# Own PSUM banks for y of the first four blocks, one product pair for the factors of all blocks, and a new order

## The chip, the cores and the metric

The kernel runs on one core of a Trainium2 chip. The metric is the device time in microseconds of one execution. A core has a matrix engine (PE), a vector engine (DVE), a scalar engine (ACT), a general engine (POOL), and a queue engine (SP) that here issues every transfer (DMA). Each engine works through its own list of instructions in order and waits on semaphores that the others raise.

## What is computed

Three steps follow one another: a chunked state-space scan over 32 sequences (batch 4, heads 8) of 768 tokens, and two gated feed-forward layers over the 3072 tokens.

```python
for c in range(nc):                                    # the scan, chunk by chunk
    L = np.exp(cum[:, :, :, None] - cum[:, :, None, :]) * causal
    M = np.einsum('bhin,bhjn->bhij', Cc, Bc) * L
    y_intra = np.einsum('bhij,bhjd->bhid', M, xc)
    y_inter = np.einsum('bhin,bhnd->bhid', Cc, state) * np.exp(cum)[:, :, :, None]
    y[:, :, sl] = y_intra + y_inter
    Bx = np.einsum('bhjn,bhjd->bhjnd', Bc, xc) * np.exp(cum[:, :, -1:] - cum)[:, :, :, None, None]
    state = np.exp(np.sum(la, axis=-1))[:, :, None, None] * state + np.sum(Bx, axis=2)

h = x @ w_in                                           # layer 1: 256 -> 2048 -> 256
x = (h * (1.0 / (1.0 + np.exp(-h)))) @ w_out
h = x @ w_in                                           # layer 2, other weights
g = (a[0] + a[1]*h + a[2]*h**2 + a[3]*h**3) / (1.0 + abs(b[0])*abs(h) + abs(b[1])*h**2 + 1e-06)
out = g @ w_out
```

The weights of both layers come as 64-bit floats. Operands of the layers are split into a high and a low part, and each product is taken as three (high by high, high by low, low by high).

## The kernel before, in words

The 3072 tokens are 24 blocks of 128. The scan runs block by block; layers 1 and 2 run over six groups of four blocks (512 tokens), and for each group over 16 slices f of 128 hidden units. Each slice is six products of 128x512 for h (`in_proj`) and six for the sum acc (`out_proj`). All products go through one helper, so every PE row of the profile has line 402.

The start of the program: la, cum and con (constants) are loaded; la is clipped (DVE, L478) and its logarithm taken (ACT, L479). `decays` makes eG and eL, per-token factors for each block, from products of la with cum (L496, L499, L513); it is called for blocks 0 to 3 and, later, for 4 to 23. `factors` makes Ea, factors along the chunk: for blocks 0 to 2 directly (lab, L565 or L567; product; exponential L552), for the others in two products for all blocks whose exponentials T (L552) are written to dre in DRAM (L576) and come back, repeated over partitions, as Ea (L688). Ea of block 3 comes alone, the others in groups of two to four.

One block of the scan: its data is loaded into tok (L675, six buffers); POOL multiplies B by eL (L713); DVE or POOL multiply C by Ea (L720, then L724); Gm is eG times a triangle (L699). PE makes CB (eight records of 64x128 from tok) and the chunk sums U (eight of 32x64), both in att, a PSUM tile of four banks. DVE makes M from CB and Gm (L768) and the states S (L787, L789). PE then makes y from M and x (x16) and from C and S (one or two times x8); ACT rounds it to y1h (L893) and DVE keeps the rest as y1l (L896). From block 5 on (`ALONE`), one "visit" of PE makes CB and U of the next block and y of this one. In att, each of CB, U and y has two places, by the block's parity, in the same four banks.

One weight slice of layer 1: the raw 64-bit words are loaded into wraw (L590, three buffers); ACT makes a scaled copy wv (L603), DVE shifts and joins the bits (L609, L611), ACT takes the high part w (L627) and POOL or DVE the low part (L631). Layer 2's weights take the same path into wraw, are written to DRAM (w2s) and reloaded later.

In a layer, ACT applies the gate (T, L976), ACT or POOL take gh (L935, L937) and DVE or POOL take gl (L941). PSUM has eight banks: four for att, two for acc, two for h (a ring that decays, factors and the layers share). Warm-up products of zeros (23 of 128x512, bf16) go into a bank of acc.

The order on every engine is set by a list scheduler in the kernel (`Plan.run`): each operation has a key, an estimated length and dependencies; at each step it takes, among those that could start first, the one with the lowest key. The keys come from a table, `first`, of one line per operation: its number, its key, and the time before which it isn't placed. `wr` and `rd` name the PSUM banks that an operation writes or reads, for the planner's estimate of when it can start. Names such as tok_101 carry a running number that differs between two versions: in the kernel before, tok_101, 106, 112 and 124 are blocks 0 to 3; in the changed one tok_113, 130, 133 and 143.

## Time and profile before

| what | us |
|---|---|
| median of 3 runs | 592.51 (591.71 to 593.67) |
| the profiled execution, its own time | 591.67 |
| its span, first to last instruction | 589.8 |
| PE busy | 577.5 |
| DVE busy | 434.7 |
| ACT busy | 405.7 |
| POOL busy | 301.5 |

The page gives busy time by engine over the whole span, then the chain of work that ended last, and the groups of instructions. PE is at 98% of the span, so what matters is where it waits and what it does before layer 1 begins. The views by stretch and in order of time show that.

### The profile page before, as it was taken

What the parts mean: (1) busy time and instruction counts of PE and PEld (TensorE: products, weight loads), DVE (VectorE), ACT (ScalarE), POOL (GpSimd) and SP (SyncE); (2) the same over time, 40 slices, a digit from 0 to 9 for tenths busy, and PEclk for the clock granted to TensorE, in tenths of its full rate; (3) what the DMA queues carried; (4) which work ended last, traced back from release to release, by engine and by line L of the source; (5) the groups of instructions that cost most, each with busy time, mean ns of one, the idle gap of its engine ahead of it and who ended that gap; (6) DMA issues with size and microseconds to landing.
All of it is one profiled execution on the core that took longest, in us unless ns stands there. A gap on an engine that the chain in (4) does not pass through costs nothing.

```text
span 589.8 us, 11914 instructions
## 1 busy us (share of the span) xinstructions
PE 577.5 (98%) x4589; PEld 463.8 (79%) x4589; DVE 434.7 (74%) x722; ACT 405.7 (69%) x728; POOL 301.5 (51%) x328
## 2 busy tenths in 40 slices
PE   7799999999999999999999999999999999999997
PEld 4477777777888888888888888888888888888885
DVE  4899999888522222222124999999999999999995
ACT  4466666456433544444446899989999999999994
POOL 4354416541112100100102788888888888888883
PEclk9799999999999999999999999999999999999999
DMA  7876566876300000000047500000000000000000
GB/s 249 260 238 229 199 198 241 293 234 221 144 1 0 1 0 1 1 1 0 1 138 230 203 1 1 37 1 1 36 1 2 37 1 0 36 2 2 36 2 36
DMA packets 16200, 48.84 MB, mean 83 GB/s; under 512 B 1872, under 2 KB 2960, under 8 KB 16144
## 3 DMA queue, kind: packets, MB, share of 16 engines
q1 hardware_dynamic: 16144, 48.09, 24.0%
q8 instruction: 36, 0.59, 0.4%
q14 instruction: 20, 0.16, 0.1%
HBM read 36.44 MB, written 11.64 MB: 82 GB/s over the span
## 4 chain that ended last, share of the span: by engine, by line
PE 87%; DVE 6%; DMA 3%; ACT 2%; SPq 1%; issue 1%; DVEq 0%; ACTq 0%
PE acc L402 42%; PE h L402 34%; PE b L402 8%; PE att L402 3%; DMA wraw<-in_w_dram 2%; DVE wv L611 1%; DVE w L631 1%; DVE wv L609 1%; DMA Ea<-dre 1%; DVE M L768 1%; ACT wv L603 1%; SPq L675 0%; DVE y1l L896 0%; ACT T L976 0%; DVE S L789 0%
## 5 line engine op out<-in xcount | busy, mean ns | idle before, releaser
L402 PE MATMUL h<-y1h,w 128*128 128x512 f32 x636 | 216.9, 391 | 0.4 <-ACT y1h L893 0.3
L402 PE MATMUL acc<-gh,w 128*128 128x512 f32 x768 | 207.1, 391 | 0.0
L402 PEld LDWEIGHTS acc<-gh,w 128*128 128x128 f32 x768 | 143.1, 188 | 30.6 <-ACT wraw L1100 0.3
L941 DVE TENSOR_TENSOR gl<-T,gh 128x512 fp32r<-128x512 f32 x85 | 59.7, 705 | 115.6 <-ACT gh L935 90.4
L402 PEld LDWEIGHTS h<-y1h,w 128*128 128x128 f32 x636 | 119.3, 188 | 26.9 <-ACT y1h L893 0.8
L941 POOL TENSOR_TENSOR gl<-g,gh 128x512 fp32r<-128x512 f32 x95 | 122.8, 1295 | 19.4 <-ACT gh L935 16.5
L402 PE MATMUL h<-y1l,w 128*128 128x512 f32 x318 | 123.9, 390 | 0.3 <-DVE y1l L896 0.3
L402 PE MATMUL acc<-gl,w 128*128 128x512 f32 x384 | 118.5, 389 | 0.0
L976 ACT ACTIVATE T<-h 128x512 f32<-128x512 f32 x96 | 57.1, 596 | 80.6 <-PE h L402 78.3
L937 POOL TENSOR_SCALAR gh<-T 128x512 fp32r<-128x512 f32 x21 | 14.1, 670 | 167.0 <-PE acc L402 122.9
L402 PEld LDWEIGHTS acc<-gl,w 128*128 128x128 f32 x384 | 72.1, 188 | 15.2
L1042 POOL TENSOR_SCALAR tok<-T,abt 128x512 f32<-128x512 f32 x96 | 74.3, 774 | 9.3 <-ACT T L1034 8.7
L1045 DVE SCALAR_TENSOR_TENSOR b<-T,absb,b 128x512 f32<-128x512 f32 x96 | 71.6, 751 | 2.6 <-ACT T L1034 1.7
L1063 DVE SCALAR_TENSOR_TENSOR g<-tok,abt,b 128x512 f32<-128x512 f32 x96 | 71.2, 743 | 0.9 <-ACT b L1057 0.3
L1054 ACT ACTIVATE b<-b,lnb 128x512 f32<-128x512 f32 x96 | 64.5, 673 | 8.4 <-DVE b L1045 8.0
L402 PEld LDWEIGHTS h<-y1l,w 128*128 128x128 f32 x318 | 59.7, 188 | 12.7 <-DVE y1l L896 0.6
L935 ACT ACTIVATE gh<-T 128x512 fp32r<-128x512 f32 x75 | 47.4, 632 | 26.1 <-PE acc L402 25.4
L1057 ACT ACTIVATE b<-b 128x512 f32<-128x512 f32 x96 | 57.4, 599 | 0.5
L1051 DVE SCALAR_TENSOR_TENSOR tok<-T,abt,h 128x512 f32<-128x512 f32 x63 | 46.8, 744 | 0.7
L402 PE MATMUL b<-y1h,w 128*128 128x512 f32 x132 | 45.8, 389 | 0.0
L1048 DVE TENSOR_TENSOR h<-tok,h 128x512 f32<-128x512 f32 x63 | 43.4, 689 | 0.1
L1038 ACT ACTIVATE b<-h,abt 128x512 f32<-128x512 f32 x63 | 42.3, 672 | 0.2 <-DVE tok L1051 0.2
(68 smaller groups left out, 619.1 us busy)
## 6 DMA issues: line engine op xcount, KB each, us to landing
wraw<-in_w_dram SPq DMA_DIRECT2D x32, 512.0 KB, 4.5
tok<-in_tok_dram SPq DMA_DIRECT2D x24, 384.0 KB, 4.5
w2s<-wraw SPq DMA_DIRECT2D x16, 512.0 KB, 3.6
w<-w2s SPq DMA_DIRECT2D x16, 512.0 KB, 4.8
out_dram<-wraw SPq DMA_DIRECT2D x12, 256.0 KB, 2.1
Ea<-dre SPq DMA_DIRECT2D x3, 268.0 KB
Ea<-dre SPq DMA_DIRECT2D x2, 201.0 KB
cum<-in_consts_dram SPq DMA_DIRECT2D x1, 192.0 KB, 2.4
```

What stands on the lines that cost most here:

```text
L402: PE.matmul(out, lhsT, rhs, start=start, stop=stop)
L935: ACT.activation(gh.t[:, 0:W], g.t[:, 0:W], AF.Copy)
L941: eng.tensor_tensor(gl.t[:, 0:W], g.t[:, 0:W], gh.t[:, 0:W], op=ALU.subtract)
L976: ACT.activation(T.t[:, 0:w], h.t[:, 0:w], AF.Silu)
L1038: ACT.activation(c.t[:, 0:W], h.t[:, 0:W], AF.Abs, scale=abt[:, 4:5])
L1042: POOL.tensor_scalar(t1.t[:, 0:W], s.t[:, 0:W], abt[:, 3:4], abt[:, 1:2], op0=ALU.mult, op1=ALU.add)
L1045: DVE.scalar_tensor_tensor(c.t[:, 0:W], s.t[:, 0:W], absb[:, 1:2], c.t[:, 0:W], op0=ALU.mult, op1=ALU.add)
L1048: DVE.tensor_tensor(h.t[:, 0:W], t1.t[:, 0:W], h.t[:, 0:W], op=ALU.mult)
L1051: DVE.scalar_tensor_tensor(t1.t[:, 0:W], s.t[:, 0:W], abt[:, 2:3], h.t[:, 0:W], op0=ALU.mult, op1=ALU.add)
L1054: ACT.activation(c.t[:, 0:W], c.t[:, 0:W], AF.Ln, bias=lnb)
L1057: ACT.activation(c.t[:, 0:W], c.t[:, 0:W], AF.Exp, scale=-1.0)
L1063: DVE.scalar_tensor_tensor(g.t[:, 0:W], t1.t[:, 0:W], abt[:, 0:1], c.t[:, 0:W], op0=ALU.add, op1=ALU.mult)
```

## The change

- A second PSUM tile, front, takes the four banks that h and acc have later. It holds y of blocks 0 to 3 (columns 0 to 255 of each bank, 64 per block), the products of decays (columns from 256 of banks 0 to 2), the products of factors (banks 0 and 1, columns 0 to 133) and the warm-up products (bank 3, columns from 256). CB and U stay in att. When the first h is made, `layers_begin` gives front back and makes acc and h in its place; the first h therefore waits for every reader of front, the warm-up products among them.
- `decays` runs once for all 24 blocks: two products of 128x192 for eG, one for eL.
- y of the first four blocks waits for the exponentials of all factors, since these lie in the same columns.
- Warm-up is 27 pairs of 128x256.
- The planner keeps ACT and DVE from reading one bank at the same time, and has other lengths for the transfers of dre and Ea.
- The table of keys is a new one, so that all engines have another order up to the end of layer 1. From the last groups of layer 1 on, PE's order is the same in both.
- Over the program, POOL makes 12 of the 24 Gm instead of 8, and DVE 2 more of the tok products, 2 more low parts of layer 1's weights, 1 more of layer 2's and 2 more gl.

```diff
@@ -47,10 +47,9 @@
-    warm=23,
+    warm=27,
...
-    late=275.632,
...
@@ -72,110 +71,109 @@
     first=[
-        (69, -141.23, 0.0), (231, -130.88, 0.0), (181, -127.55, 0.0), (81, -123.22, 0.0), (86, -119.72, 0.0), (62, -119.71, 0.0), (227, -118.33, 0.0), (103, -114.97, 0.0),
...
+        (166, -223.78, 0.0), (189, -216.25, 0.0), (470, -211.24, 0.0), (457, -174.69, 0.0), (7, -172.83, 0.0), (8, -167.32, 0.0), (431, -165.03, 0.0), (250, -163.48, 0.0),
...
@@ -297,7 +295,7 @@
             for b in op.rd:
-                t = max(t, wrote.get(b, 0.0))
+                t = max(t, wrote.get(b, 0.0), read_by.get((b, "ACT" if e == "DVE" else "DVE"), 0.0))
...
@@ -316,6 +314,7 @@
             for b in op.rd:
                 was_read[b] = max(was_read.get(b, 0.0), op.end + self.LAT[e])
+                read_by[b, e] = op.end + self.LAT[e]
...
@@ -341,7 +340,7 @@
-            kw = {"SB": {}, "PS": dict(space=bass.MemoryType.PSUM), "DR": dict(space=bass.MemoryType.DRAM)}[space]
+            kw = {"SB": {}, "PS": dict(space=bass.MemoryType.PSUM, side="right"), "DR": dict(space=bass.MemoryType.DRAM)}[space]
...
@@ -435,9 +434,17 @@
     ring("h", 2, 512, space="PS")
-    acc_t = [fixed(f"acc{d}", [P, 512], space="PS") for d in range(2)]
-
-    pool(2, "PS")
+    acc_t = []
+    first_pool = ExitStack()
+    first_ps = first_pool.enter_context(tc.tile_pool(name="PSfirst", bufs=1, space=bass.MemoryType.PSUM, side="right"))
+    front = first_ps.tile([P, 4, 512], F32, tag="front", name="front")
+
+    def layers_begin():
+        if not acc_t:
+            first_pool.close()
+            acc_t.extend(fixed(f"acc{d}", [P, 512], space="PS") for d in range(2))
+            pool(2, "PS")
+
@@ -456,6 +463,8 @@
 
     R_acc = [Ring(1), Ring(1)]
     R_cb, R_psu, R_yt = Ring(2), Ring(2), Ring(2)
+    R_em, R_y0 = Ring(2), Ring(BLOCKS[0])
+    FRONT = range(4, 8)
     O_Y, O_U = 2 * P, 2 * P + 2 * CH
 
 
@@ -481,42 +490,35 @@
 
     o_eG, o_eL = {}, {}
 
-    def decays(first, last, key, after):
-        cols = slice(first * H, last * H)
-        w = (last - first) * H
-        ps = new("h")
+    def decays(key):
+        w = NTB * H
 
         def f_eg_mm():
-            ps.t = ps.make()
             for p in range(SPC):
-                mm(ps.t[:, p * w : p * w + w], cum.t[:, p * P : (p + 1) * P], la[:, cols], True, True)
+                mm(front[:, p, 256 : 256 + w], cum.t[:, p * P : (p + 1) * P], la, True, True)
 
         def f_eg_min():
-            v = ps.t[:, 0 : SPC * w].rearrange("p (a b) -> p a b", a=SPC)
-            DVE.tensor_scalar(eG[:, :, cols], v, 80.0, None, op0=ALU.min)
+            DVE.tensor_scalar(eG, front[:, 0:SPC, 256 : 256 + w], 80.0, None, op0=ALU.min)
 
         def f_eg_exp():
-            ACT.activation(eG[:, :, cols], eG[:, :, cols], AF.Exp)
-
-        a = add({"PE": (max(0.4, SPC * w / 580), f_eg_mm)}, key, [o_ln, ld_cum] + after, new=[ps], use=[cum], cols=4 * SPC * w, big=False)
-        a = add({"DVE": (c_dve(SPC * w), f_eg_min)}, key, [a], use=[ps])
-        a = add({"ACT": (c_act(SPC * w), f_eg_exp)}, key, [a])
-        for n in range(first, last):
-            o_eG[n] = a
-        ps_c = new("h")
+            ACT.activation(eG, eG, AF.Exp)
+
+        a = add({"PE": (0.68, f_eg_mm)}, key, [o_ln, ld_cum], use=[cum], wr=[4, 5], cols=4 * SPC * w, big=False)
+        b = add({"DVE": (c_dve(SPC * w), f_eg_min)}, key, [a], rd=[4, 5])
+        a = add({"ACT": (c_act(SPC * w), f_eg_exp)}, key, [b])
 
...
@@ -524,35 +526,38 @@
         POOL.memset(zeros.t[:, 0:DM], 0.0)
 
     o_zero = add({"POOL": (0.3, f_zero)}, 0.0, new=[zeros])
-    spare = R_acc[1].new(lambda: acc_t)
+    o_warm = []
     for i in range(int(K["warm"])):
 
         def f_warm():
             z = zeros.t.bitcast(mybir.dt.bfloat16)
-            mm(acc_t[1], z[:, 0:P], z[:, 0:512], True, True)
-
-        add({"PE": (0.215, f_warm)}, 99.0, [o_zero], use=[zeros, spare], cols=512, after=K["warm0"] + K["warmstep"] * i)
-
-    decays(0, 4, 1.0, [])
+            for _ in range(2):
+                mm(front[:, 3, 256:512], z[:, 0:P], z[:, 0:256], True, True)
+
+        o_warm.append(
+            add({"PE": (0.215, f_warm)}, 99.0, [o_zero], use=[zeros], wr=[7], cols=512, after=K["warm0"] + K["warmstep"] * i)
+        )
+
+    o_bulk = []
     o_ee, o_dre, dre = {}, [], fixed("dre", [H, NTB, P + R6], space="DR")
     Ea = fixed("Ea", [P, NTB * (P + R6) + 48])
     Ev = Ea[:, 0 : NTB * (P + R6)].rearrange("p (n e) -> p n e", n=NTB)
 
     def factors(la_cols, key, after, n, use=()):
-        Ee, pe = new("T") if n is None else None, new("h")
+        Ee, pe = new("T") if n is None else None, R_em.new(None)
+        q = R_em.turns.index(pe) % 2
         out = lambda: Ev[:, n, :] if Ee is None else Ee.t[:, 0 : P + R6]
 
         def f_em():
-            pe.t = pe.make()
-            mm(pe.t[:, 0 : P + R6], la_cols(), difs, True, True)
+            mm(front[:, q, 0 : P + R6], la_cols(), difs, True, True)
 
         def f_ee():
             if Ee:
                 Ee.t = Ee.make()
-            ACT.activation(out(), pe.t[:, 0 : P + R6], AF.Exp)
-
-        a = add({"PE": (0.29, f_em)}, key, [o_ln, ld_con] + after, new=[pe], use=list(use), cols=4 * (P + R6))
-        return Ee, add({"ACT": (c_act(P + R6, True), f_ee)}, key, [a], new=[Ee] if Ee else [], use=[pe])
+            ACT.activation(out(), front[:, q, 0 : P + R6], AF.Exp)
+
+        a = add({"PE": (0.29, f_em)}, key, [o_ln, ld_con] + after, new=[pe], use=list(use), wr=[4 + q], cols=4 * (P + R6))
+        return Ee, add({"ACT": (c_act(P + R6, True), f_ee)}, key, [a], new=[Ee] if Ee else [], use=[pe], rd=[4 + q])
 
     for n in range(E_DIRECT):
         lab = new("lab")
@@ -575,8 +580,8 @@
             ns = slice(i * P // H, min(NTB, (i + 1) * P // H))
             nc.sync.dma_start(dre.rearrange("h n e -> n h e")[ns], Ee.t[skip * H :, 0 : P + R6])
 
-        o_dre.append(dma(K["bulk"] + 2 * i, 68e3, f_dre, [a], use=[Ee]))
-    decays(4, NTB, K["late"], [])
+        o_bulk.append(a)
+        o_dre.append(dma(K["bulk"] + 2 * i, 170e3, f_dre, [a], use=[Ee]))
 
 
     w_at, o_w = [None] * NF, [None] * NF
@@ -688,7 +693,7 @@
                     nc.sync.dma_start(Ev[:, n0:n1, :], dre[:, n0:n1, :].unsqueeze(1).broadcast_to([H, N, n1 - n0, P + R6]))
 
                 first, end = n0 * H // P, (n1 - 1) * H // P
-                o = dma(k_load, 155e3 * (n1 - n0), f_er, o_dre[first : end + 1])
+                o = dma(k_load, 160e3 * (n1 - n0) + 60e3, f_er, o_dre[first : end + 1])
                 o_ee.update(dict.fromkeys(range(n0, n1), o))
         e0 = lambda: Ev[:, n, P : P + R6]
 
@@ -811,8 +816,10 @@
     def y_parts(ns):
-        ybs = [R_yt.new(lambda: att) for _ in ns]
-        cols = [O_Y + CH * (n % 2) for n in ns]
+        early = ns[0] < BLOCKS[0]
+        ybs = [(R_y0 if early else R_yt).new(lambda: att) for _ in ns]
+        cols = [CH * n if early else O_Y + CH * (n % 2) for n in ns]
+        out = [front[:, q, :] for q in range(4)] if early else att
 
         def f_mx():
             for n, yo in zip(ns, cols):
@@ -823,7 +830,7 @@
                         for i in range(NCH):
                             ts = slice(CH * i, CH * i + CH)
                             mm(
-                                att[2 * k + i][32 * j : 32 * j + 32, yo : yo + CH], x()[ts, h * D : h * D + D],
+                                out[2 * k + i][32 * j : 32 * j + 32, yo : yo + CH], x()[ts, h * D : h * D + D],
                                 m.t[ts, h * CH : h * CH + CH], n == ns[0], n == ns[-1] and into[n][i] is None,
                             )
 
...
@@ -858,7 +865,7 @@
                 f_mx()
                 f_cs()
 
-            o_y = add({"PE": (y_len + 0.05, f_y)}, T + 5 * d, y_deps, new=ybs, use=y_use, wr=range(4), cols=y_cols, big=False)
+            o_y = add({"PE": (y_len + 0.05, f_y)}, T + 5 * d, y_deps, new=ybs, use=y_use, wr=FRONT if n < BLOCKS[0] else range(4), cols=y_cols, big=False)
             if n + 1 < min(NTB, ALONE + 1):
                 cb_alone(n + 1)
                 u_alone(n + 1)
@@ -885,8 +892,9 @@
         for n, yb, yo in zip(ns, ybs, cols):
             b, o = blk_of[n], n * P
             T, d = at[n][1:3]
-            o_xT.setdefault(b, [])
-            yv = quad[:, :, yo : yo + CH].rearrange("p (k c) i -> p k c i", k=2)
+            o_xT.setdefault(b, [] if b else o_warm + [o_eG[0], o_eL[0]])
+            banks = FRONT if n < BLOCKS[0] else range(4)
+            yv = (front if n < BLOCKS[0] else quad)[:, :, yo : yo + CH].rearrange("p (k c) i -> p k c i", k=2)
...
@@ -967,6 +974,7 @@
             h, T, wa = new("h"), new("T"), w_at[f]
 
             def f_a(f=f, h=h, wa=wa, w=w, xh=xh, xl=xl):
+                layers_begin()
                 h.t = h.make()
                 wts[f] = parts_of(wa.t)
                 in_proj(f, h.t, xh, xl, w)
@@ -975,7 +983,7 @@
                 T.t = T.make()
                 ACT.activation(T.t[:, 0:w], h.t[:, 0:w], AF.Silu)
 
-            ready = o_xT[b][2 * c0 // P : 2 * c1 // P]
+            ready = o_xT[b]
             a = add({"PE": (c_mm(w, 6), f_a)}, t0, cols=6 * w, deps=[o_w[f]] + ready, new=[h], use=[wa])
             a = add({"ACT": (c_act(w, True), f_b)}, t0 + 0.1, [a, o_tab0], new=[T], use=[h])
             o_silu.append(a)
...
```

On SP, from the first block's data on; before (L675 is a block's data, L590 a weight, L576 the factors to DRAM, L688 from there):

```order
L675 DMA tok_101<-in_tok_dram 128x768
L675 DMA tok_106<-in_tok_dram 128x768
L675 DMA tok_112<-in_tok_dram 128x768
L675 DMA tok_124<-in_tok_dram 128x768
L590 DMA wraw_138<-in_w_dram 128x512
L590 DMA wraw_152<-in_w_dram 128x512
L590 DMA wraw_175<-in_w_dram 128x512
L471 DMA abt<-in_ab_dram 128x6
L576 DMA dre<-T_191 16x8x134
L576 DMA dre<-T_197 8x8x134
L675 DMA tok_210<-in_tok_dram 128x768
L688 DMA Ea<-dre 128x1x134
```

And now, at the same place (L680 is a block's data, L595 a weight, L581 and L693 the factors):

```order
L480 DMA abt<-in_ab_dram 128x6
L595 DMA wraw_102<-in_w_dram 128x512
L680 DMA tok_113<-in_tok_dram 128x768
L680 DMA tok_130<-in_tok_dram 128x768
L680 DMA tok_133<-in_tok_dram 128x768
L680 DMA tok_143<-in_tok_dram 128x768
L680 DMA tok_159<-in_tok_dram 128x768
L581 DMA dre<-T_169 16x8x134
L680 DMA tok_189<-in_tok_dram 128x768
L581 DMA dre<-T_187 8x8x134
L595 DMA wraw_216<-in_w_dram 128x512
L693 DMA Ea<-dre 128x1x134
```

One weight moved ahead of all blocks, the other two behind six blocks or further back.

On ACT, before, from the last direct factor to the second decays (L603 is a weight's first step):

```order
L552 ACTIVATE Ea<-h_149 128x134
L603 ACTIVATE wv_183<-wraw_138 128x512
L552 ACTIVATE T_191<-h_178 128x134
L552 ACTIVATE T_197<-h_185 128x134
L603 ACTIVATE wv_208<-wraw_152 128x512
L603 ACTIVATE wv_233<-wraw_175 128x512
```

And now, from the first weight (L608) to y1h (L901) of the first three blocks:

```order
L608 ACTIVATE wv_136<-wraw_102 128x512
L504 ACTIVATE eG<-eG 128x384
L514 ACTIVATE eL<-front 128x192
L557 ACTIVATE Ea<-front 128x134
L570 ACTIVATE lab_154<-la 128x128
L557 ACTIVATE Ea<-front 128x134
L632 ACTIVATE w_10_162<-wv_136 128x512
L557 ACTIVATE Ea<-front 128x134
L557 ACTIVATE T_169<-front 128x134
L557 ACTIVATE T_187<-front 128x134
L390 ACT_TABLE_LOAD
L608 ACTIVATE wv_314<-wraw_216 128x512
```

The first weight's step moved ahead of eG, eL and all exponentials of the factors.

On DVE, before, from the first row that needs Ea of block 3 on (L609 and L611 are a weight's bit steps, L631 its low part; the last two y1l of the first group come 18 rows behind the first):

```order
L720 TENSOR_TENSOR tok_124<-tok_124,Ea 128x256
L611 SCALAR_TENSOR_TENSOR wv_233<-wraw_175,wv_233 128x512
L724 TENSOR_TENSOR tok_124<-tok_124,Ea 128x256
L631 TENSOR_TENSOR w_30_330<-wv_233,w_30_330 128x512
L609 TENSOR_SCALAR wv_208<-wv_208 128x512
L789 SCALAR_TENSOR_TENSOR S_362<-S_260,Ea,att 128x64
L768 TENSOR_TENSOR M_368<-att,Gm_242 128x512
L896 TENSOR_TENSOR y1l<-att,y1h 128x2x128
L789 SCALAR_TENSOR_TENSOR S_380<-S_362,Ea,att 128x64
L896 TENSOR_TENSOR y1l<-att,y1h 128x2x128
```

And now, the whole of it, from there to the last y1l of the first group (L614 and L616 are the bit steps):

```order
L725 TENSOR_TENSOR tok_143<-tok_143,Ea 128x256
L904 TENSOR_TENSOR y1l<-front,y1h 128x2x128
L773 TENSOR_TENSOR M_340<-att,Gm_262 128x512
...
L773 TENSOR_TENSOR M_425<-att,Gm_345 128x512
L794 SCALAR_TENSOR_TENSOR S_430<-S_343,Ea,att 128x64
L904 TENSOR_TENSOR y1l<-front,y1h 128x2x128 x2
L614 TENSOR_SCALAR wv_314<-wv_314 128x512
L616 SCALAR_TENSOR_TENSOR wv_314<-wraw_216,wv_314 128x512
L725 TENSOR_TENSOR tok_268<-tok_268,Ea 128x256
L904 TENSOR_TENSOR y1l<-front,y1h 128x2x128
```

Weight steps moved out from between Ea and the last y1l; the M of three blocks moved in.

## Rows read from the trace of the kernel before

**Rows 1.** The page's busy times by engine.

```profile
PE 577.5 (98%) x4589; PEld 463.8 (79%) x4589; DVE 434.7 (74%) x722; ACT 405.7 (69%) x728; POOL 301.5 (51%) x328
```

**Rows 2.** Busy time (and instructions) per engine by stretch, clock, DMA share, GB/s.

```profile
0.00:29.07 29.07, 22.31 (x462) 12.81 (x462) 18.22 (x41) 12.14 (x27) 12.45 (x22) 0.88 0.79 252
29.07:77.05 47.98, 46.49 (x795) 35.77 (x796) 45.82 (x91) 32.79 (x59) 22.52 (x19) 1.00 0.65 219
77.05:100.00 22.95, 22.65 (x329) 17.26 (x335) 20.70 (x41) 14.49 (x28) 10.81 (x12) 1.00 0.69 237
```

**Rows 3.** ACT in order of time: start, length, row, idle time before and releaser.

```profile
10.96 0.68 ACT L603 ACTIVATE wv<-wraw 128x512 f32<-128x512 f32 x1 [3.12 <-DMA wraw<-in_w_dram]
11.54 0.43 ACT L552 ACTIVATE T<-h 128x134 f32<-128x134 f32 x2
...
13.39 0.66 ACT L603 ACTIVATE wv<-wraw 128x512 f32<-128x512 f32 x1 [0.51 <-DMA wraw<-in_w_dram]
```

**Rows 4.** SP's issues in order of time, then the chain of waits.

```profile
11.83 1.80 SPq L576 DMA_DIRECT2D dre<-T  x2
...
14.65 1.28 SPq L688 DMA_DIRECT2D Ea<-dre  x2
...
14.65 3.89 DMA Ea<-dre
```

**Rows 5.** DVE in order of time, from Ea to y1l of the fourth block.

```profile
18.64 0.43 DVE L720 TENSOR_TENSOR tok<-tok,Ea 128x256 f32<-128x256 f32 x1 [0.91 <-DMA Ea<-dre]
...
22.10 0.69 DVE L768 TENSOR_TENSOR M<-att,Gm 128x512 f32<-128x512 f32 x1 [0.52 <-ACT y1h L893]
...
28.32 0.74 DVE L896 TENSOR_TENSOR y1l<-att,y1h 128x256 fp32r<-128x256 f32 x2
...
76.37 0.68 DVE L631 TENSOR_TENSOR w<-wv,w 128x512 fp32r<-128x512 f32 x1
```

**Rows 6.** DVE's groups, 29.07 to 77.05: count, busy us, mean ns, idle before.

```profile
L611 DVE SCALAR_TENSOR_TENSOR wv<-wraw,wv 128x512 uint32<-128x512 uint32 x13 | 9.7, 754 | 0.0
L609 DVE TENSOR_SCALAR wv<-wv 128x512 uint32<-128x512 uint32 x13 | 6.9, 534 | 0.3 <-ACT wv L603 0.3
L631 DVE TENSOR_TENSOR w<-wv,w 128x512 fp32r<-128x512 f32 x8 | 6.6, 819 | 0.6 <-ACT w L627 0.6
L941 DVE TENSOR_TENSOR gl<-T,gh 128x512 fp32r<-128x512 f32 x9 | 6.1, 683 | 0.1
L724 DVE TENSOR_TENSOR tok<-tok,Ea 128x256 f32<-128x256 f32 x8 | 5.1, 662 | 0.0
L768 DVE TENSOR_TENSOR M<-att,Gm 128x512 f32<-128x512 f32 x7 | 4.7, 683 | 1.0 <-ACT y1h L893 1.0
L720 DVE TENSOR_TENSOR tok<-tok,Ea 128x256 f32<-128x256 f32 x9 | 4.2, 488 | 0.0
L789 DVE SCALAR_TENSOR_TENSOR S<-S,Ea,att 128x64 f32<-128x64 f32 x13 | 3.5, 272 | 0.1
L699 DVE TENSOR_TENSOR Gm<-eG,con 128x512 f32<-128x512 f32 x4 | 2.7, 681 | 0.0
L896 DVE TENSOR_TENSOR y1l<-att,y1h 128x256 fp32r<-128x256 f32 x6 | 2.5, 414 | 0.0
```

**Rows 7.** The chain of waits in block 1: groups of six products around one visit.

```profile
139.35 1.36 PE acc L402 x6
140.71 1.44 PE att L402 x93
142.15 2.94 PE acc L402 x12
```

**Rows 8.** PE in order of time, then PE by stretch with the granted clock.

```profile
16.85 0.68 PE L402 MATMUL att<-M,tok 64*32 64x64 f32 x32 [3.47 <-DVE S L789]
...
17.00:18.00 1.00, 1.00 (x63) 0.50 1.05 337
...
24.00:25.00 1.00, 0.58 (x49) 1.00 0.52 171
```

## The prediction, made before the changed kernel was run

> **What bounds the kernel now.** I read the page first: PE is busy for 577.5 of 589.8 us [rows 1]. Then busy time by stretch [rows 2]: up to 29.07 us PE has 22.31 of 29.07, and what it has there is warm-up products and small attention products. From 29.07 to 77.05, PE 46.49 and DVE 45.82 of 47.98. From there to 100, PE is idle for 0.3. So the end is set by three things: when layer 1 begins (it waits for the last y1l, which ends at 29.06 [rows 5]), by what PE loses until it has all sixteen weights of layer 1, and by PE's own work afterwards, which neither version changes (layer 2 has the same order on PE in both). Between 29.07 and 77.05 PE loses 1.5 us, and DVE 2.2: both are near their limit, and whoever gains on one of them has the other next.

> Why does layer 1 begin at 29? The chain of waits goes back to one transfer [rows 3, 4]. ACT works in order. Its exponential T of the factors for the blocks from 3 on (L552, 11.54) stands behind wv, which waits for the first weight, landed at 10.96 behind four blocks of tok. SP issues dre at 11.83, Ea of block 3 at 14.65, and that lands at 18.54. DVE then needs from 18.64 to 29.06 for 20 instructions with hardly a gap [rows 5], among them seven of weight conversion (L609, L611, L631), before the fourth block's y1l is out.

> **The change, part by part.**

> *Clock and sums.* Everything is reckoned in the profiled run: 591.67 us with a span of 589.8, against a median of 592.51; a saving in the span is taken off the median.

> *First transfers.* SP now issues cum, la, con, abt, one weight, then five tok. By their shapes (a weight 512 KB, a tok 384, cum 192, con 99, la 96) 902 KB are queued up to the end of that weight, where before it was 2435 KB (with four tok ahead). Between the landings of the first and the third weight (10.96 and 13.39 [rows 3]) 1024 KB came in 2.43 us, 421 KB per us; 1533 KB fewer is 3.6 us earlier, so it lands at 7.3. That is an extrapolation down to a time when the queue was still filling: bounds 6.3 and 8.3.

> *The chain to dre.* Nine ACT instructions now stand between that landing and the end of T: wv, eG, eL, three Ea, one lab, one w, T. Wv takes 0.58 from start to start (10.96 to 11.54 [rows 3]) and w is like it; the other seven are of 128 to 384 columns, bounded by 0.2 (the pair of T took 0.43) and 0.4; I take 0.25, since most are of T's size. That is 2.9 us: T done at 10.2, dre 1.6 earlier than 11.83. From there the queue is as before: two dre, a tok and a weight where two tok stood, then Ea. I leave that at 18.54 - 11.83 = 6.7 us, so Ea of block 3 lands at 16.9. That one product pair makes eG and eL of all blocks saves two products and two exponentials that layer 1 does not wait for: nothing for the end.

> *From Ea to layer 1.* DVE has 14 instructions from tok_143 to the last y1l: two L720, four y1l, three M, two S, one Gm, one L609, one L611 of the sizes of [rows 6]. By those means 2x0.488 + 4x0.414 + 3x0.683 + 2x0.272 + 0.681 + 0.534 + 0.754 = 7.2 us. The 20 of before by the same means (three L720, three L611, two L724, two L631, two L609, three S, one M, four y1l) are 10.9 and took 10.42; so 6.9. Layer 1 begins at 23.8, 5.3 us earlier. That y of four blocks has its own banks is what lets U and CB of later blocks run ahead of it on PE; on DVE it removes the short waits of M for y1h (0.52 us at 22.1 [rows 5]), which are inside this 6.9 or not: 0.5 either way.

> *From there to the sixteenth weight.* This is where the gain is given back. Before, 91 DVE instructions stand between the last y1l and the last L631 of layer 1; their busy times add up to 52.2 (52.0 in [rows 6], 0.2 for one copy) and they took 47.98 (they overlap a little). After, the 91 rows from wv_506 to w_60 are: 15 L609, 14 L611, 11 L631, 12 gl, 9 L724, 6 L720, 5 M, 3 Gm, 11 S, 5 y1l. At the same means: 8.0 + 10.6 + 9.0 + 8.2 + 6.0 + 2.9 + 3.4 + 2.0 + 3.0 + 2.1 = 55.2, hence 50.7 us: DVE begins with two weights converted instead of four. It ends at 74.5 instead of 77.05: 2.55 earlier. POOL has 16 instructions beside it instead of 19 [rows 2]. Where POOL runs, DVE's rows with two SBUF operands get longer: L724 takes 0.662 against y1l's 0.414 at the same 256 columns, L631 0.819 against M's 0.683, L611 0.754, L720 0.488. The excess is 8x0.25 + 8x0.14 + 13x0.07 + 9x0.07 = 4.7 us; three nineteenths of that, 0.7, I take off. [...]

> *What PE has done by then.* One group of six products is 1.36 us, a visit 1.44 plus 0.22 on the group behind it [rows 7]. Before, up to the sixteenth weight: 26 groups and 7 visits, 47.0 us. After: 28 groups and 5 visits, 46.4: 0.6 is still owed. PE alone could be there at 23.8 + 46.4 = 70.2, so DVE with its 74.5 (73.8 with the 0.7) sets it, not PE.

> *Sum.* 2.55 + 0.7 - 0.6 = 2.65 us. **589.9 us.** Afterwards PE hardly waits before, and no more is expected after: the later visits (y9 on) move into block 1's products, with the same number of instructions.

> *Other edits.* 54 warm-up products of 256 columns for 23 of 512 run while PE has nothing else to do until about 13 us; the order puts all of them ahead of the second CB. Costed at nothing: PE waits for others in that time, before for 3.47 us at a stretch [rows 8]. The release of front before the first h adds a wait of PE for y1l of the fourth block, which h needs anyway. DVE and ACT may no longer be planned in the same bank at once: that only moves rows.

> **The rivals.**

> *PE, not DVE, is next (586 to 588).* If the stretch of 4.7 us by POOL is gone, w_60 is there at 70, as early as PE. Then the 5.3 of the earlier start stays: 587.2 if PE loses 1.5 on the way, as before, 585.9 if it loses next to nothing. For it: POOL has less beside DVE, and DVE's first rows after 23.8 are a new mix. Against it: DVE had only 2.2 us of idle in 48, and the order still puts a conversion ahead of nearly every group of h.

> *The clock is low when layer 1 begins (592.5).* [...] After, all warm-up products come early, and from about 13.5 to 18 PE waits for Ea again, with no filler behind. If the clock falls there, the first groups of layer 1 run at 2.7 instead of 1.36 us for up to the rest of a 7 us stretch: some 3.5 us of PE. That alone would be hidden by DVE's lateness, but ACT's wv of weights 4 to 6 stands behind the silu of the third h, so DVE waits with it: 2.5 us lost, no gain left. [...]

> *Block 1 becomes DVE's turn (592.3).* The visits of blocks 9 to 20 now lie in block 1's stretch. From the sixteenth weight to M of block 15, PE has 23 groups and six visits, 41.3 us, and DVE 72 instructions, 42.7 by the means of [rows 6], 39.2 at before's overlap: 2.1 us of slack. DVE a tenth slower than that costs 1.8, and the short waits between M and y1h (seven visits, 0.5 each at most) as much again: 2.4 in the middle. Against it: before, PE waited for just 0.3 us from 77.05 to 100, with DVE 20.7 of 22.95 us busy [rows 2].

> *ACT holds the fourth y1h back (595).* The order puts wv_314 ahead of all y1h, and the L627 of w_18 ahead of the fourth. If weight 2, queued behind both dre and a tok, lands late, y1h, y1l and so layer 1 wait. My chain has it at about 17, with Ea. Layer 1 starting 1 us later is 1 us; from 28 on it's slower than before, and with a landing at 23, 4.5 after Ea's 18.54 of before, it begins at 29.5: 595. Against it: the transfers of before landed 3.9 to 6 us after their issue, and this one is issued near 12.8.

> *It does nothing (592.5).* PE waits for one late y1l in both, and the new banks serve nobody.

> **How the numbers follow.** Forecast 0.36, PE next 0.24, clock 0.14, block 1 0.10, ACT 0.12, nothing 0.04. A measurement here can tell about 0.3%, 1.8 us: faster below 590.7, slower above 594.3. The forecast's own spread (588 to 591.3, from the weight's landing and 0.2 to 0.4 per ACT row) gives 0.05 to "same". Faster 0.31 + 0.24 = 0.55, same 0.05 + 0.14 + 0.10 + 0.04 = 0.33, slower 0.12. The range goes from 586 to 594: it leaves out most of the ACT case and a tail below.

> **What would show it.** After: the first weight at ACT by about 7.3; dre issued near 10.2; Ea of block 3 by 16.9; h from about 23.8; the last L631 of layer 1 (w_60) near 74, with DVE over 93% busy up to there; PE idle 3 to 4 us between 24 and 74; no idle of PE from 80 on. Wrong would be: granted clock 0.50 past 24 us, the step behind L724 at 0.42 instead of 0.66 us on DVE, or PE idle after 80 with DVE as the releaser.

## The result: 0.6% slower, and the profile after

The changed kernel takes 597.03 us (median of 20 runs, 592.45 to 599.41), the kernel before 593.29 us on the same chips (20 runs, 591.71 to 596.61). The ratio is 1.0057, with a 95% interval from 1.0041 to 1.0074: slower by more than the 0.3% that can be told. The profiled run of after took 597.9 us with a span of 596.1. The profiled run of before is one of the fastest of its kernel and that of after lies 0.9 us above its median, so the spans differ by 6.3 us where the medians differ by 3.7.

The page's busy times and the three stretches (up to the first h, up to the end of the sixteenth weight, up to 100 us) answer to [rows 1] and [rows 2]. Columns: length, busy us (instructions) of PE, weight load, DVE, ACT, POOL, then granted clock, DMA share, GB/s.

```profile
PE 580.5 (97%) x4614; PEld 467.9 (78%) x4614; DVE 433.5 (73%) x724; ACT 407.7 (68%) x730; POOL 288.4 (48%) x321
...
0.00:32.67 32.67, 22.25 (x470) 14.79 (x471) 14.25 (x32) 10.32 (x22) 11.93 (x22) 0.81 0.66 201
32.67:81.15 48.48, 47.34 (x626) 36.99 (x627) 44.27 (x92) 33.13 (x61) 14.38 (x18) 0.95 0.68 226
81.15:100.00 18.85, 18.85 (x262) 14.83 (x261) 16.59 (x32) 11.52 (x22) 6.52 (x8) 1.00 0.60 220
```

Layer 1 begins at 32.67 us, 3.6 later than before, not 5.3 earlier. (Before, the first product of h already starts at 28.32, but the second waits for the last y1l until 29.11; the 3.6 us count from there.) DVE has had 14.25 us of work by then and waited for the rest. In the second stretch it is PE that is full (47.34 of 48.48) while DVE has 4.2 us to spare. The second stretch has a mean clock of 0.95 where [rows 2] has 1.00.

ACT and SP up to the fourth y1h (start, length, row, idle before and releaser) answer to [rows 3, 4]:

```profile
6.52 0.66 ACT L608 ACTIVATE wv<-wraw 128x512 f32<-128x512 f32 x1 [1.61 <-DMA wraw<-in_w_dram]
...
11.38 0.28 ACT L557 ACTIVATE Ea<-front 128x134 f32<-128x134 f32 x1 [0.83 <-PE front L401]
12.33 0.28 ACT L557 ACTIVATE T<-front 128x134 f32<-128x134 f32 x1 [0.67 <-PE front L401]
14.16 0.28 ACT L557 ACTIVATE T<-front 128x134 f32<-128x134 f32 x1 [1.55 <-PE front L401]
...
19.83 0.67 ACT L608 ACTIVATE wv<-wraw 128x512 f32<-128x512 f32 x1 [4.08 <-DMA wraw<-in_w_dram]
21.65 0.38 ACT L901 ACTIVATE y1h<-front 128x256 fp32r<-128x256 f32 x1 [1.15 <-PE front L401]
24.13 0.38 ACT L901 ACTIVATE y1h<-front 128x256 fp32r<-128x256 f32 x1 [2.09 <-PE front L401]
28.99 0.38 ACT L901 ACTIVATE y1h<-front 128x256 fp32r<-128x256 f32 x1 [4.48 <-PE front L401]
31.26 0.63 ACT L632 ACTIVATE w<-wv 128x512 fp32r<-128x512 f32 x1 [1.88 <-DVE wv L616]
31.79 0.36 ACT L901 ACTIVATE y1h<-front 128x256 fp32r<-128x256 f32 x1
```

```profile
12.64 0.65 SPq L581 DMA_DIRECT2D dre<-T  x1
...
14.47 0.69 SPq L581 DMA_DIRECT2D dre<-T  x1
15.22 0.40 SPq L595 DMA_DIRECT2D wraw<-in_w_dram  x1
15.72 0.64 SPq L693 DMA_DIRECT2D Ea<-dre  x1
```

The first weight is there at 6.52, even earlier than forecast. Then ACT waits for PE before each of the five exponentials of the factors, and T is done at 14.4. PE in the same time, and from y of the second block to the first h:

```profile
8.25 0.50 PE L401 MATMUL front<-con,lab 128*128 128x134 f32 x2 [0.42 <-ACT eL L514]
9.11 0.60 PE L401 MATMUL front<-T 128*128 128x256 bf16 x4 [0.37 <-ACT Ea L557]
10.08 0.81 PE L401 MATMUL front<-con,lab 128*128 128x134 f32 x2 [0.37 <-ACT Ea L557]
...
21.22 0.39 PE L401 MATMUL front<-T 128*128 128x256 bf16 x2
...
23.16 0.46 PE L401 MATMUL front<-M,tok 64*32 64x64 f32 x32 [0.92 <-DVE M L773]
23.54 0.47 PE L401 MATMUL front<-tok,S 32*32 32x64 f32 x32
...
24.56 0.42 PE L401 MATMUL front<-M,tok 64*32 64x64 f32 x23
27.84 0.44 PE L401 MATMUL front<-M,tok 64*32 64x64 f32 x9 [2.85 <-issue]
...
30.22 0.68 PE L401 MATMUL front<-M,tok 64*32 64x64 f32 x32 [0.94 <-DVE y1l L904]
30.83 0.67 PE L401 MATMUL front<-tok,S 32*32 32x64 f32 x32
32.67 0.80 PE L401 MATMUL h<-y1h,w 128*128 128x512 f32 x1 [1.17 <-DVE y1l L904]
```

Three things are seen here. From 8 to 13 us PE waits for ACT's exponential again and again (0.37 to 0.42 us each time) before a product into front, warm-up products (front<-T) too, though the exponential reads one bank and the product goes to another: front is one tile. The y of the fourth block waits 0.94 us for y1l of the third, in the same tile. And in the middle of y of the third block PE stands, that is, it is idle, for 2.85 us with no releaser ("issue").

The granted clock, in PE's own stretches (length, busy, clock, DMA share, GB/s):

```profile
12.00:13.00 1.00, 0.63 (x4) 0.50 0.00 0
...
24.00:25.00 1.00, 0.84 (x40) 1.00 0.96 194
26.00:27.00 1.00, 0.00 (x0) 0.92 0.90 226
28.00:29.00 1.00, 1.00 (x57) 0.50 0.50 195
...
36.00:37.00 1.00, 1.00 (x4) 0.50 0.90 317
37.00:38.00 1.00, 1.00 (x27) 0.96 0.91 316
```

It is low twice. From 10 to 16 us it is 0.50, while PE and ACT wait for each other. Behind the stand it is 0.50 again, up to 37 us, so the first twelve products of h take 5.05 us (32.67 to 37.72) instead of 2x1.36 [rows 7]: 2.3 us. Put together on PE: 3.6 us of later start, 2.3 of low clock, 1.1 for a second stand at 56.62, 0.6 for the two CB (32 pairs of weight load and matmul) that before ran ahead of h and now run behind it, less the 1.8 us that PE idled from 29.07 to 100 us before [rows 2]: 5.8 of the 6.3 us between the spans. Behind 100 us PE idles 4.1 us, 3.7 before, which is most of the rest. This is the account of two profiles; the medians differ by less.

### The profile page after: what moved, and what is told of

It is laid out like the page before. It is cut to its first block, busy times and chain, and to the rows that moved or that the text cites. A ratio compares the mean times of both kernels' runs of the same rounds, so it can differ in the third digit from the quotient of the medians.

```text
span 596.1 us, 11965 instructions
## 1 busy us (share of the span) xinstructions
PE 580.5 (97%) x4614; PEld 467.9 (78%) x4614; DVE 433.5 (73%) x724; ACT 407.7 (68%) x730; POOL 288.4 (48%) x321
## 3 DMA queue, kind: packets, MB, share of 16 engines
q1 hardware_dynamic: 16144, 48.09, 23.8%
## 4 chain that ended last, share of the span: by engine, by line
PE 93%; DMA 3%; DVE 2%; issue 1%; ACT 1%; SPq 0%; POOL 0%; POOLq 0%
PE acc L401 43%; PE h L401 35%; PE b L401 8%; PE att L401 4%; PE front L401 3%; DMA wraw<-in_w_dram 2%; DMA w2s<-wraw 1%; DVE wv L614 0%; DVE M L773 0%; DVE y1l L904 0%; DVE gl L949 0%; ACT y1h L901 0%; ACT wv L608 0%; ACT Ea L557 0%; DVE wv L616 0%
## 5 line engine op out<-in xcount | busy, mean ns | idle before, releaser
L401 PE MATMUL h<-y1h,w 128*128 128x512 f32 x636 | 219.6, 395 | 1.2 <-DVE y1l L904 1.2
L949 DVE TENSOR_TENSOR gl<-T,gh 128x512 fp32r<-128x512 f32 x87 | 61.3, 704 | 112.5 <-ACT gh L943 94.2
L945 POOL TENSOR_SCALAR gh<-T 128x512 fp32r<-128x512 f32 x17 | 10.5, 620 | 179.6 <-PE acc L401 116.4
L943 ACT ACTIVATE gh<-T 128x512 fp32r<-128x512 f32 x79 | 49.7, 631 | 26.7 <-PE acc L401 26.1
```

The lines of the kernel that those rows point to most:

```text
L401: PE.matmul(out, lhsT, rhs, start=start, stop=stop)
L943: ACT.activation(gh.t[:, 0:W], g.t[:, 0:W], AF.Copy)
L949: eng.tensor_tensor(gl.t[:, 0:W], g.t[:, 0:W], gh.t[:, 0:W], op=ALU.subtract)
```

## The experiments

All were timed against the kernel before on the same chip, with 6 or 12 runs each. "h" is the start of the first product of layer 1 in the profiled run, "12 h" the time that the first twelve take (left out for e9 and e10, where the ten stand among them).

```
                       median   ratio to before [95%]     h      12 h
kernel before          593.29                             28.32
changed kernel         597.03   1.0057 [1.0041, 1.0074]   32.67  5.05
e1  own tiles          594.41   1.0027 [1.0009, 1.0046]   27.91  4.34
e2  54 pairs more      594.98   1.0044 [1.0023, 1.0065]   28.49  4.42
e3  weight 2 late      597.06   1.0079 [1.0055, 1.0103]   33.62  4.94
e4  filled             596.77   1.0066 [1.0044, 1.0089]   31.44  5.39
e5  Ea late            596.98   1.0065 [1.0045, 1.0085]   30.08  5.49
e6  early y            593.36   1.0007 [0.9987, 1.0027]   29.79  5.02
e7  early y, Ea late   591.62   0.9980 [0.9966, 0.9995]   27.02  5.21
e8  e7 filled          594.73   1.0026 [1.0007, 1.0045]   28.93  4.59
e9  before, 10 more    593.89   1.0023 [1.0008, 1.0037]   27.74
e10 changed, 10 more   600.14   1.0129 [1.0099, 1.0159]   31.16
e11 filled, 512 wide   595.65   1.0042 [1.0019, 1.0066]   27.83  3.01
e12 fill at the edge   597.53   1.0092 [1.0065, 1.0119]   31.17  4.59
```

**e1: front as four tiles until the first y.**

```
-    front = first_ps.tile([P, 4, 512], F32, tag="front", name="front")
+    own = [first_ps.tile([P, 512], F32, tag=f"own{q}", name=f"own{q}") for q in range(4)]
...
-            mm(front[:, q, 0 : P + R6], la_cols(), difs, True, True)
+            mm(own[q][:, 0 : P + R6], la_cols(), difs, True, True)
```

> The changed kernel, with the four banks of front as four tiles of their own until the first y (factors in two, the products for eG in one, eL and the warm-up products in one), and front as one tile only from there; same order on every engine. Theory A (PE and ACT take turns because every product into front waits for the last reader of front, whichever bank it reads): the last exponential T starts near 10.5 us instead of 14.16, both dre are issued by 11.5, weight 2 is at ACT by 17 instead of 19.83, and the first h comes 1.5 to 3 us earlier than 32.67; the time falls by 1 to 3 us. Theory B (ACT's chain is simply long, or PE at half clock is what takes the time): T stays past 13, and the time within 0.5 us. The 2.85 us in which PE stands in the middle of y of the third block should stay in both.

ACT of e1, where the waits for PE are gone or short:

```profile
9.03 0.27 ACT L565 ACTIVATE T<-own 128x134 f32<-128x134 f32 x1
9.72 0.28 ACT L565 ACTIVATE T<-own 128x134 f32<-128x134 f32 x1 [0.41 <-PE own L401]
16.46 0.66 ACT L616 ACTIVATE wv<-wraw 128x512 f32<-128x512 f32 x1 [5.16 <-DMA wraw<-in_w_dram]
```

T is at 9.72 instead of 14.16, the first h 4.8 us earlier, more than theory A said. The order is the same on every engine, so the waits for a whole tile did cost time. But PE's clock differs too: it is 1.00 up to 16 us in e1. In e4, which is the changed kernel up to there and has 1.00 as well, T comes at 12.55:

```profile
12.55 0.28 ACT L557 ACTIVATE T<-front 128x134 f32<-128x134 f32 x1 [0.92 <-PE front L401]
```

So of the 4.4 us some 2.8 are the tile's and 1.6 the clock's, which theory B had named. The medians fall by 2.6 us, the ratio by 0.3 points (1.8 us; the intervals just overlap): the stand is still there (3.06 us, again in y of the third block), and so is the low clock behind it (0.50 from 26 to 30 us).

**e2: the same warm-up columns in twice as many pairs.**

```
-            for _ in range(2):
-                mm(front[:, 3, 256:512], z[:, 0:P], z[:, 0:256], True, True)
+            for c in (256, 384, 256, 384):
+                mm(front[:, 3, c : c + 128], z[:, 0:P], z[:, 0:128], True, True)
```

> The changed kernel with each warm-up product of 256 columns as two of 128: the same columns, but 54 more pairs of weight load and matmul on PE ahead of the y products. Theory A (PE stands for 2.85 us because it has run to the end of the instructions that are loaded, at its 349th pair in the kernel after and its 348th in the kernel before): it stands again at about the 349th pair, which is now 54 pairs earlier in the program, at the first state products of y of the second block, not in y of the third. Theory B (it stands there for what runs beside it, or for something that y of the third block needs): it stands again behind 23 of the 32 products of y of the third block. Time within 1.5 us of the changed kernel in both.

PE of e2, around its stand:

```profile
20.91 0.35 PE L401 MATMUL front<-tok,S 32*32 32x64 f32 x17
22.36 0.47 PE L401 MATMUL front<-tok,S 32*32 32x64 f32 x15 [1.10 <-issue]
```

The stand has moved to y of the second block, behind pair 349, where theory A put it: it went with the instruction number (1.10 us here, 2.85 at pair 349 in after). By the ratios e2 is 0.8 us faster than the changed kernel, within what was allowed. The kernel before has the stand too, at its pair 348:

```profile
25.75 0.34 PE L402 MATMUL att<-tok,S 32*32 32x64 f32 x15 [0.28 <-issue]
```

Counted in program order, the stands of before, after and the experiments in the first 62 us lie, where the trace has every record, at pairs 220 to 221, 348 to 349, 475 to 476, 858 to 859 and 986 to 987, whatever is computed there: 128 pairs, 256 instructions, apart, or three times that, within two pairs. Such a place is called an edge below. (The list in the expectation of e5 has 605 too; no trace shows a stand there. Four pauses without a releaser lie elsewhere: 0.65 us at 19.66 in after, 0.42 at 24.47 in before, 0.19 and 0.82 in e7; at the same products e6 and e9 wait for POOL.) The instruction queue on the page of after, and the DMA queues from 24 to 25 us and from 25 to 25.2 (packets, MB, share):

```profile
q8 instruction: 36, 0.59, 0.4%
...
q1 hardware_dynamic: 94, 0.19, 95.7%
...
q1 hardware_dynamic: 19, 0.02, 65.9%
q8 instruction: 1, 0.02, 40.4%
```

36 packets with 0.59 MB are 16.4 KB each, and 2x4614 instructions on PE are 256 for each packet. One comes at 25.1, behind the end of PE's last product at 24.98, and PE goes on at 27.84. In the kernel before the packet came at 23.1, while PE worked on ten warm-up products of 512 columns, and PE came to the edge only at 25.47 and stood 0.28 us. In the runs PE goes on 2.2 to 2.9 us behind the packet (3.2 once, in a stand of 0.24). From one edge to the next, 128 pairs of y, U and CB took PE 3.4 us here (21.6 to 24.98), and the packet came 3.5 us behind the first of the two. That PE waits for this packet is inferred from these times and from the count of 256.

**e3: weight 2 behind all y1h.**

```
+    for op, mark in ((exp, yh), (bits1, yl), (bits0, yl), (hi, plan.ops[conv[2]]), (lo, hi)):
+        behind(op, mark)
```

> The changed kernel with the conversion of weight 2 (L608, L614, L616, L632, L636) put behind y1h and y1l of the fourth block on ACT and DVE. Rival 'ACT holds y1h back': the first y1h starts near 18.7 instead of 21.65 and the first h is 2 to 3 us earlier. Theory A (PE's last warm-up products into front hold the first y1h until 21.6 whatever ACT does, and further on the y of each block waits for the y1h and y1l of the one ahead): the first y1h stays at 21.6, and the first h comes 0.3 to 0.5 us earlier, which the second group of h gives back; time within 0.7 us.

```profile
21.15 0.38 ACT L901 ACTIVATE y1h<-front 128x256 fp32r<-128x256 f32 x1 [5.33 <-PE front L401]
```

The first y1h is at 21.15 instead of 21.65, and it waits for PE, whose last warm-up products into front end at 21.1. ACT's wv of weight 2 did not hold it, here and in after, where the clock was 0.50 up to 16 us. It does in the runs where PE was ahead: in e2, e4 and e10 those products end at 18.0 to 18.2, and y1h starts right behind wv, at 18.72, 19.14 and 20.35. So the rival holds in part, and e3, in whose run PE was late, can't tell how much it is worth. h came later (33.62), because the stand was 4.19 us in this run; time as the changed kernel.

**e4: nine products of 128 columns ahead of y of the fourth block, and nine behind it.**

```
+                for _ in range(k if n == BLOCKS[0] - 1 else 0):
+                    mm(quad[:, 0, O_Y : O_Y + P], z[:, 0:P], z[:, 0:P], True, True)
```

> The changed kernel with nine products of 128 columns ahead of y of the fourth block and nine behind it, into unused columns of the other PSUM tile, where PE waits for y1l (0.94 and 1.17 us). Theory A (the low clock at the start of layer 1 comes from PE's idle times between 25 and 32.7 us): the granted clock is back at 1.00 by 34 to 35 us instead of 37, the first twelve products of h take 3.5 to 4.2 us instead of 5.05, and the time falls by 1 to 2 us. Theory B (DVE, not PE, sets the pace there, as the prediction had it): the first products are faster but the time falls by less than 0.5 us.

Missed. The waits were filled, but PE stood three times (1.00, 2.27 and 1.59 us, at pairs 221, 349 and 476): the added pairs had moved the third edge into y of the fourth block. The clock was 0.50 up to 36 us. The run says nothing on the clock's price.

**e5: two Ea transfers later.**

```
+    for n0 in (12, 9):
+        behind(er[n0], er[4])
```

> The changed kernel with two of the three Ea transfers that SP issues together at 19.0 us (blocks 9 to 15, 474 KB) put behind the next tok and Ea, so that the DMA engines have less to do between 20 and 25 us. In the runs so far PE stands at fixed instruction numbers (its pairs 221, 349, 477, 605, 861, 989: every 128 pairs of weight load and matmul, that is every 256 instructions), and goes on 2.3 to 2.8 us after a 16 KB packet on the instruction queue. Theory C (that packet is asked for when PE passes the edge before, at 21.6 us for the one at pair 349, and waits on the DMA engines behind the data): the packet comes at 22 to 23.5 us instead of 25.09, PE stands for less than 1.3 us at pair 349 instead of 2.85, and the time falls by 1 to 3 us. Theory D (the packet's time hangs on PE's own progress, not on data transfers): still 3.5 us behind the edge at pair 221, still 2.5 to 4 us of standing, time within 0.7 us.

The DMA share from 22 to 24 us fell from 0.83 to 0.52, the packet came at 23.1, 3.2 us behind the edge before it instead of 3.5, and PE stood for 2.00 us instead of 2.85. The time is the same. Theory C is not borne out; in e8, e11 and e12 that delay was 1.8 to 2.0 us, in e11 with a DMA share of 0.95 (16 to 18 us), in e12 with the transfers as in the changed kernel. Theory D's 2.5 to 4 us of standing did not come either. What sets the delay stays open.

**e6 and e7: e1, and the path to the first y1h cleared; e7 with the transfers of e5.**

```
-            for _ in range(2):
+            for _ in range(0 if front_t else 2):
...
+    behind(exp, y1hs[1])
+    behind(hi, y1hs[3])
```

Neither computes the twelve warm-up products behind the first y, whose results nobody reads.

> The kernel of the run with four tiles of their own for factors and decays, and beside that: the twelve warm-up products that stand behind the first y are left out, wv of weight 2 goes behind the second y1h on ACT, and w of weight 2 behind the fourth. Theory A (the first y1h waits for PE's last warm-up products into front and then for wv, and the y of the next block, M and y1l wait behind it): the first y1h starts at 13.6 to 14.5 us instead of 17.03, and the first h at 24.5 to 26.5 instead of 27.91; the time is below that of the kernel before by 0 to 3 us if every us at the start of layer 1 is one at the end, that is, if PE sets the pace from there. Theory P (DVE sets the pace from there, as the prediction had it): the same early start, but the time falls by less than half of what the start gains against the run with own tiles alone. A stand of 2 to 4 us at PE's pair 349 is expected in both; the pair is now at the beginning of the state products of y of the third block.

> Both edits above together: own tiles, no warm-up products behind the first y, weight 2 behind the second y1h, and the two Ea transfers later. Theory C: the stand at pair 349 is under 1.3 us, the first h comes at 23 to 25 us, the time is 2 to 5 us below that of the kernel before. Theory D: as the run before it in this call, within 1 us.

The first y1h is at 13.80 in e6 and 13.47 in e7, as said. h did not follow in e6 (29.79): PE stood for 1.51 and 2.76 us. In e7 the second stand was short. PE had waited 2.21 us for M just before it (0.91 in e6), and the packet came 3.4 us behind the edge before it (4.6 in e6):

```profile
21.98 0.41 PE L401 MATMUL front<-tok,S 32*32 32x64 f32 x2
22.74 0.67 PE L401 MATMUL front<-tok,S 32*32 32x64 f32 x30 [0.35 <-issue]
...
27.02 0.80 PE L401 MATMUL h<-y1h,w 128*128 128x512 f32 x1 [1.00 <-DVE y1l L915]
```

E7 is the one kernel that measures below both: 591.62 us, 0.2% below the kernel before (0.05 to 0.34%), less than the 0.3% that can be told. Against e6 it gains 1.7 us with one transfer order; that the packet came sooner for fewer bytes is not shown (e5).

**e8, e11, e12: products of no use where PE stands or waits.** E8 is e7 with eleven of 384 columns ahead of y of the second block and e4's eighteen. E11 is e1 with the ACT and SP order of e7, warm-up products of 512 columns (21 pairs fewer), fourteen of 384 columns ahead of y of the third block, and e4's. E12 is the changed kernel with those fourteen alone.

```
+                if n == 2:
+                    fill(front[:, 3, 128:512], 384, 14)
```

> The kernel of the run with own tiles, no warm-up products behind the first y, weight 2 behind the second y1h and the two Ea transfers later, with products of no use added where PE waits: eleven of 384 columns ahead of y of the second block (there PE waited 2.21 us for M), nine of 128 columns ahead of y of the fourth block (0.93 us) and nine behind it (1.00 us). In the run without them the granted clock was 0.50 from 19 to 31 us. Theory A (the clock falls for these waits, and the first groups of h pay for it): the clock stays at 1.00 up to the first h or falls only for the stand at an instruction edge, the first twelve products of h take 2.7 to 3.5 us instead of 4.7, and the time is 1.0 to 2.5 us below that of the run without them, so 2 to 4 us below the kernel before. Rival: the added pairs move the instruction edge forward to y of the third block, PE stands longer there and the clock falls all the same: time within 0.7 us of the run without them.

> Four tiles of their own for factors and decays; weight 2 behind the second y1h; two Ea transfers later; the warm-up products ahead of the first y as one of 512 columns instead of two of 256 (21 pairs fewer, so that the instruction edge at pair 349 comes at the end of y of the third block and the one at 477 behind y of the fourth); the twelve behind the first y as in the changed kernel; and products of no use: fourteen of 384 columns ahead of y of the third block, where PE stood for the instruction edge, nine of 128 ahead of y of the fourth and nine behind it. Theory (h can't begin before some 26.5 us, for the instruction pages of the y products; what is left to win is the clock): first h at 26.3 to 27.5 us, granted clock 1.00 there, the first twelve products of h in under 3.2 us, and a time 1.5 to 3.5 us below the kernel before. Rival (the filling products take PE's time without keeping the clock, or an edge falls in a worse place): time within 1 us of the kernel before or above it.

> The changed kernel with fourteen products of 384 columns of no use ahead of y of the third block, just before the place where PE stood for 2.85 us at the instruction edge, and nothing else. Theory A (the stand lets the clock fall, and the first groups of h pay for it): the stand shrinks to under 1 us, the first h stays at 32 to 33.5 us, the clock there is 1.00 or back by 35 us, and the time falls by 1 to 2.5 us. Rival (the page of instructions comes later by as much as the filling takes, or the waits behind it bring the clock down as well): time within 0.7 us of the changed kernel, or above it.

In e8 the clock had fallen by 16 us, so the eleven took 3.68 us (the fourteen of e12, at 1.00, 2.44) and y of the second block came 1.7 us later than in e7. In e12 the stand at pair 349 was gone, but PE stood 0.99 us at pair 476, with a wait of about 1 us for y1l on either side, and the clock fell again (0.50 from 32 to 34 us). Of the changed orders only e11 had the clock at 1.00 when h began (27.83) and for the whole of its twelve products, which took 3.01 us. Then PE waited for DVE:

```profile
30.45 0.39 PE L401 MATMUL h<-y1h,w 128*128 128x512 f32 x1
32.79 1.12 PE L401 MATMUL att<-tok 32*64 32x128 f32 x32 [1.95 <-DVE tok L736]
```

DVE was on the bits of weight 3 and the tok of the next blocks without a gap from 28.2. So a start near 28 at full clock does meet DVE, for one wait; the clock fell behind it (0.50 from 34 to 36 us), and the 2 us were lost again. (At the same product e1, e2, e3, e6 and e8 wait 0.31 to 0.73 us for DVE.) None of the three gained: by the ratios e8 is 2.7 us slower than e7, e12 2.1 slower than the changed kernel, and e11 0.9 slower than e1.

**e9 and e10: ten products more in the second group of h.**

```
+                for _ in range(10 if (b, f) == (0, 1) else 0):
+                    mm(h.t[:, 0:w], wts[f][0][:, 0:P], xh[:, 0, :], True, True)
```

> The kernel before, with the first product of the second group of h made eleven times instead of once: ten products of 512 columns more on PE at the start of layer 1, 2.1 us by the 1.36 us that six take. Theory P (as the prediction had it, DVE sets the pace from the start of layer 1 to the sixteenth weight): at most 0.7 us of it is seen at the end. Theory E (PE sets the pace and keeps what it loses): 1.8 to 2.2 us at the end.

> The changed kernel with the same ten products more. Theory P (DVE sets the pace): at most 0.7 us at the end. [...]

By the spans the kernel before ends 2.0 us later (591.8 against 589.8), the changed kernel 2.6 (598.7 against 596.1); by the ratios 1.4 us (0.5 to 2.2) and 4.3 (1.0129 less 1.0057, about 2 us either way). Theory P allowed 0.7, which the interval of e9 alone does not exclude. The traces of before and of e9 do: the 72nd silu of ACT, far behind the sixteenth weight, comes 2.04 us later:

```profile
252.61 0.60 ACT L976 ACTIVATE T<-h 128x512 f32<-128x512 f32 x1 [1.18 <-PE h L402]
...
254.65 0.60 ACT L978 ACTIVATE T<-h 128x512 f32<-128x512 f32 x1 [1.18 <-PE h L402]
```

PE sets the pace from layer 1 on, in both, but for single waits such as e11's, and what it loses there it keeps. The 4.3 us of e10 are more than theory E of e9 said. Its ten products took longer (the twelve in a row from 33.45 take 4.07 us, those of e9 2.91); where the rest comes from is open.

## Why the prediction was wrong, step by step

*First transfers.* Forecast 7.3, measured 6.52 at ACT. Right.

*The chain to dre: the step that failed first.* "Nine ACT instructions ... 2.9 us: T done at 10.2" summed ACT's lengths as if they followed each other. Measured 12.64 and 14.47 for the two dre. Between the exponentials stands a product that writes into the same tile, and it waits for the exponential ahead (0.37 us); e1 took that away and had T at 9.72, near the forecast, though partly by luck: its chain from the weight's landing took 3.6 us, not 2.9, and the landing was 0.8 earlier. What the prediction left out is that front is one tile: these waits went by the tile, whichever bank was read or written (some 2.8 us of them in all, by e1 and e4). The low clock of this profile (0.50 from 10 to 16 us) made each turn longer, by some 1.6 us in all (e4).

*"54 warm-up products ... Costed at nothing".* They took part in that exchange (two of PE's three waits for Ea stand ahead of such a product), and those behind the first y held the first y1h until 21.65. Without them, and with wv of weight 2 moved behind, it starts at 13.8 (e6); with wv moved and the products kept, at 15.58 (e11); with neither, at 17.03 (e1). Their cover was named, what waits for them in turn was not.

*From Ea to layer 1.* Forecast 16.9 for DVE's first row with Ea of block 3, and 6.9 us from there. That row (the second L725 of the pair below) starts at about 21.1, and up to the end of the last y1l at 32.62 it took 11.5:

```profile
20.75 0.75 DVE L725 TENSOR_TENSOR tok<-tok,Ea 128x256 f32<-128x256 f32 x2
...
32.19 0.43 DVE L904 TENSOR_TENSOR y1l<-front,y1h 128x256 fp32r<-128x256 f32 x1 [0.63 <-ACT y1h L901]
```

The path was another one as well. Followed back from the first h, the chain of waits holds no transfer: up to the first y1h it is PE's products into front,

```profile
14.79 2.10 PE front L401 x10
...
17.27 1.74 PE front L401 x56
```

and from there y1h, y1l, M, y and the stand in turn. Three parts of the 11.5 us can be named: 2.85 us of PE's stand, which the prediction had not among its causes though the trace of before holds a 0.28 us one; the wait of y for y1h and y1l of the block ahead (0.94 us at the fourth); and w of weight 2 in front of the fourth y1h. The last is the rival "ACT holds the fourth y1h back"; it cost 0.3 us (PE's products end at 31.5, y1h starts at 31.79); at the first y1h it was PE, not ACT, that was waited for in this profile, and ACT in others (e3).

*"DVE ... sets it, not PE".* Wrong. The stretch took 48.5 us, near the 50.7 forecast, but not for the reason given: DVE was busy for 44.27 us of it, its rows add up to 4.5 us less than the 55.2 reckoned, and it idled 4.2 us, PE 1.1. The 4.5 us are most of the 4.7 put down to POOL, as the rival "PE next" had it: L729 takes 0.415 us where 0.662 was reckoned and L636 0.688 where 0.819, but L725 0.490, where 0.488 was. That POOL beside it is enough to lengthen a row is not shown: in the trace of before L724 takes 1.52 us at 72.11, beside POOL's gl, and 0.42 at 70.60, beside POOL's tok. In the changed kernel:

```profile
L729 DVE TENSOR_TENSOR tok<-tok,Ea 128x256 f32<-128x256 f32 x9 | 3.7, 415 | 0.0
```

E9 shows the same for the kernel before: PE's work, not DVE's, is what the end waits for. What had looked like DVE near its limit (45.82 of 47.98) was an engine fed by PE.

*The clock rival* came true in kind: 0.50 at the start of layer 1, 2.3 us on the first twelve products. It was priced as an alternative, while it came on top of the late start, and it did not come with the cause named (idle while waiting for Ea): the clock was 1.00 from 17 to 26 us, 0.92 from 26 to 27, inside the stand from 24.98 to 27.84, then 0.50 up to 37, and 0.96 from 37 to 38, while the products of h follow one another. That is 10 us at 0.50, where the forecast's 7 lie between the two clocks of [rows 8]. What the low clock costs at the end is not shown by a run of its own, since every filling moved something else too.

*Later.* Block 1 did not become DVE's turn: PE has no idle from 81.15 to 100.

## What to carry to other kernels

Ask of every operand in a shared tile who read it last, in program order: a bank of its own bought no overlap here, where the waits went by the tile, and tiles of their own brought T some 2.8 us forward (e1, e4). Count PE's instructions, not only its time: here PE stood at places 256 of them apart, for 2.85 us where the last 256 had taken 3.4 us, and behind that the clock was 0.50 and twelve products of h took 5.05 us (3.01 at 1.00 in e11). To learn which engine sets the pace, add work to one of them, in the kernel before already: DVE's busy share near the limit did not tell, ten products more on PE (2.0 us later at the end, by the spans of e9) did.
